# Four-layer attention kernel: one key block of each unit of the last layer has its exponentials computed on VectorE

## Chip, core and metric

The kernel runs on one core of a Trainium2 chip. The metric is the time of one execution on the device, in microseconds; the median of several executions is given. A profile is the record of one execution.

## The reference

Four layers follow each other on x, 2,048 rows of 640 numbers in bf16. Each adds to x an attention over its layer norm; layers 0 and 2 use a sliding window of 256 keys ("A"), layers 1 and 3 attend to all 2,048 keys ("B"). There are 32 heads of 20.

```python
def _B_ref(x, wqkv, wo):
    B, S, D = x.shape
    H = 32
    Dh = D // H
    qkv = (lambda x, *d: x.transpose(*d))((x @ wqkv).reshape(B, S, 3, H, Dh), 2, 0, 3, 1, 4)
    q, k, v = qkv[0], qkv[1], qkv[2]
    scores = jnp.einsum("bhqd,bhkd->bhqk", q, k) * (Dh ** -0.5)
    p = _softmax(scores, axis=-1)
    o = jnp.einsum("bhqk,bhkd->bhqd", p, v)
    return (lambda x, *d: x.transpose(*d))(o, 0, 2, 1, 3).reshape(B, S, D) @ wo
...
x = A_x
x = x + _A_ref(_layernorm(x, axis=-1), A_wqkv, A_wo)
x = x + _B_ref(_layernorm(x, axis=-1), B_wqkv, B_wo)
x = x + _A_ref(_layernorm(x, axis=-1), A_wqkv, A_wo)
x = x + _B_ref(_layernorm(x, axis=-1), B_wqkv, B_wo)
```

For the change one thing matters: every score of layer 3, 32 x 2,048 x 2,048 of them, needs an exponential.

## The kernel before, in words

**Units and banks.** The queries are split into NC = 4 chunks of C = 512, the heads into G = 8 groups of four. A unit (class Unit, L602) is a layer, a chunk c and a group g. In a full layer it has 16 key blocks of 128 keys, and for each block four banks, one per head j of the group: 64 banks of 128 keys x 512 queries, each as large as one PSUM bank. Layer 3's chunk 0 is split into two parts, which belong to the woven stage before; its chunks 1 to 3 are 24 whole units and are the end of the program.

**Scores, exponentials, values.** The main loop (L926) makes one tile of banks per tick. Score matmuls (L953) write it to PSUM: even ticks to banks 0 to 2, odd ticks to banks 3 to 5, or 3 to 6 if the tile has four banks. The four heads lie in different strips of 32 rows. One ScalarE instruction (L971) takes the exponential of the whole tile from PSUM to bf16 in SBUF, into a buffer pt of three banks, or, for four banks, into a slot of ka_all, whose 18 rows layer 3 no longer needs for keys (KA // 4 = 4 slots in turn). Two or three ticks later value matmuls (L1021) accumulate the four heads of one key block into PSUM bank 7, called op. The values have a column of ones, so row 20 of each strip becomes the sum of the exponentials.

**After a unit.** finish_unit (L760) copies op to oT on VectorE (L783), which frees bank 7 for the next unit. The tail t_tail (L803) makes the reciprocals of the sums and multiplies: four matmuls L808, reciprocal L813, split L817 and L818, transpose L823 and its copy L825, four matmuls L832, product L836. After the eighth unit of a chunk t_out (L500) projects: eight times eight matmuls (L511) and an add to x (L520). For the last chunk t_before_last (L534) does seven of each eight groups ahead (L542, L550). Each step of these tasks asks take_m (L235) for a free PSUM bank; in the last layer the only one is bank 6. The four-bank tiles use it too, when no task wants it (next_tile, L893).

**Order.** The order on every engine is that of emission, fixed when the program is built. A tick emits the scores of its tile, then the exponential, then as many steps of the tasks as a credit allows (pump, L223: 0.9 per tick in the last layer), then value matmuls of an earlier tile. Engines then wait for each other by semaphores. TensorE and VectorE each run their instructions in this order.

```python
                if n_b == 4:
                    pt = ka_all[:, 4 * wide_pt : 4 * wide_pt + 4, :]
                    wide_pt = (wide_pt + 1) % (KA // 4)
                else:
                    pt = ptp.tile([P, 3, C], BF16, name="pt", tag="pt")
...
                    nc.scalar.activation(
                        out=pt[:, i:k, b0 * P :], in_=sp[:, i:k, b0 * P :],
                        func=ACT.Exp, scale=SCALE,
                    )
```

Of the kernel before, what the change touches and what calls it, by code (L numbers as in the profile page):

```python
# [8 lines left out]

BF16 = mybir.dt.bfloat16  # L10
F32 = mybir.dt.float32
ALU = mybir.AluOpType
ACT = mybir.ActivationFunctionType

P = 128
# [4 lines left out]
NT = S // P  # L20
KD = D // P
G = 8
C = 512
NC = S // C
EPS = 1e-5
SCALE = DH ** -0.5
HD = D // 2
VW = DH + 1
KA = 18
QA = 4  # L30

PARTS = {
# [6 lines left out]
def kernel(  # L39
# [10 lines left out]
    nc = tc.nc  # L50
# [11 lines left out]
    xtp = pool("xtp", 5)  # L62
# [30 lines left out]
    ka_all = big.tile([P, KA, C], BF16, name="ka", tag="ka")  # L93
    kas = [ka_all[:, n, :] for n in range(KA)]
    qas = [big.tile([P, C], BF16, name=f"qa{n}", tag=f"qa{n}") for n in range(QA)]

    ps = psp.tile([P, 8, C], F32, name="ps", tag="ps")
    op = ps[:, 7, :]
# [15 lines left out]
    def load_wop(w):  # L114
# [6 lines left out]
        out=ident[:], in_=ident[:], compare_op=ALU.not_equal, fill=1.0,  # L121
# [101 lines left out]
    def pump(credit, most):  # L223
        state["credit"] = min(state["credit"] + credit, most)
        while True:
            t = choose(state["credit"] <= 0.0)
            if t is None:
                break
            state["credit"] -= advance(t)
# [369 lines left out]
    def key_blocks(l, part):  # L599
        return part or (0, NT)  # L600

    class Unit:  # L602
        def __init__(self, l, c, g, part=None):
            self.l, self.c, self.g, self.part = l, c, g, part
            self.windowed = l % 2 == 0
            if self.windowed:
                sets = [(m, b0, subs, j) for m, b0, subs in window_banks(c) for j in range(4)]
            else:
                kcs = range(*key_blocks(l, part))
                sets = [(None, 0, [(kc, 0, 4, 0)], j) for kc in kcs for j in range(4)]  # L610
            n = len(sets)
            self.banks = [
                (self, j, m, b0, subs, i < 4, i >= n - 4, i == n - 1)
                for i, (m, b0, subs, j) in enumerate(sets)
            ]

# [143 lines left out]
    def finish_unit(u):  # L760
# [22 lines left out]
            nc.vector.tensor_copy(out=oT[:], in_=op)  # L783
        push_tail(("tail", l, c, g), t_tail(l, c, g, on, oT))

    def s_emitted(u):
        if u.windowed:
            live["qa"] -= 1
            qa_free.append(qa.pop((u.c, u.g)))
            for c in ([u.c - 1] if u.c > 0 else []) + ([u.c] if u.c == NC - 1 else []):  # L790
                live["ka"] -= 1
                ka_free.append(ka.pop((c, u.g)))
        else:
            live["kt"] -= 1
            live["qt"] -= 1
# [69 lines left out]
    with tc.manual_schedule():  # L865
# [24 lines left out]
            starts.setdefault(id(b[0]), len(tiles) + m // 3)  # L890
        banks = deque(banks[n:])

        def next_tile(t):  # L893

            if t < len(tiles):
                return tiles[t]
            size = 3
            if t % 2 and not tails and state["held"] is None and mfree[6][0] <= state["tick"]:
                if all(task.wake > state["tick"] for task in todo):
                    size = 4  # L900
            return [banks.popleft() for _ in range(min(size, len(banks)))]
# [24 lines left out]
        while ended is None or t < ended + 8:  # L926
            t += 1
            state["tick"] += 1
            n_b = 0
            if t < len(tiles) or banks:  # L930
                cur = next_tile(t)
                n_b = len(cur)
                for b in cur:
                    u = b[0]
                    if id(u) not in started:
                        started.add(id(u))
                        if u.l == 0 and u.g == 0 and u.c + 1 < NC and u.c not in pushed:
                            pushed.add(u.c)
                            push(("stats", u.c + 1), t_stats0(u.c + 1), index[0, u.c + 1, 0, None], 0.4)
                            push_layer(0, u.c + 1)  # L940
                        state["unit"] = index[u.l, u.c, u.g, u.part]
                        state["act"] = state["unit"] < woven
                        if state["early"] and not narrow(u):
                            end_early()
                        start_unit(u)
                sp = ps[:, 0:3, :] if t % 2 == 0 else ps[:, 3:7, :]
                if n_b == 4:
                    mseq[0] += 1
                    mfree[6] = (state["tick"] + 2, mseq[0])
                for n in range(2):  # L950
                    for i, (u, j, m, b0, subs, first, last, end) in enumerate(cur):
                        for kc, q0, qn, col in subs[n : n + 1]:
                            nc.tensor.matmul(  # L953
                                sp[:, i, col * P : (col + qn) * P],
                                lhsT=u.k(kc, j), rhs=u.q(j, q0, qn), start=True, stop=True,
                            )
                for b in cur:
                    if b[-1]:
                        s_emitted(b[0])
                if n_b == 4:  # L960
                    pt = ka_all[:, 4 * wide_pt : 4 * wide_pt + 4, :]
                    wide_pt = (wide_pt + 1) % (KA // 4)
                else:
                    pt = ptp.tile([P, 3, C], BF16, name="pt", tag="pt")
                i = 0
                while i < n_b:
                    b0 = cur[i][3]
                    k = i
                    while k < n_b and cur[k][3] == b0:
                        k += 1  # L970
# [4 lines that stand above are left out]
                    i = k  # L975
                for i, b in enumerate(cur):
                    pts.append((t, pt, i, b))
                load_ahead()
                r = rate(t)
                pump(r, r + 0.1)  # L980
                state["heat"] += 0.414 * n_b
                work.append((state["heat"], 1.0 * n_b))
                if woven <= state["unit"] < index[3, 1, 0, None]:
                    least = sum(w[1] for w in work) - sum(w[0] for w in work) + state["heat"]
                    keep_clock(least)
                    work[-1] = (state["heat"], 1.0 * n_b)
                state["heat"] = 0.0
            else:
                ended = t if ended is None else ended
                pump(2.0, 2.0)  # L990

            if t > 0 and masked is not None:
                cur_, pt_ = masked
                i = 0
                while i < len(cur_):
                    m, b0 = cur_[i][2:4]
                    k = i
                    while k < len(cur_) and cur_[k][2] == m:
                        k += 1
                    if m is not None:  # L1000
                        mv_ = masks[:, m, b0 * P :].unsqueeze(1).to_broadcast(
                            (P, k - i, C - b0 * P)
                        )
                        nc.vector.tensor_tensor(  # L1004
                            out=pt_[:, i:k, b0 * P :], in0=pt_[:, i:k, b0 * P :], in1=mv_,
                            op=ALU.mult,
                        )
                    i = k
            masked = (cur, pt) if n_b else None

            if len(pts) >= 4 and pts[3][0] <= t - (3 if pts[0][3][0].windowed else 2):
                group = [pts.popleft() for _ in range(4)]
                u, subs, end = group[0][3][0], group[0][3][4], group[3][3][7]
                first, last = group[0][3][5:7]
                if first and u.windowed:
                    require(("v", u.l, u.c, 0))
                    require(("v", u.l, u.c, 1))
                for n, (kc, q0, qn, col) in enumerate(subs):
                    for _, pt, i, b in group:
                        j = b[1]  # L1020
                        nc.tensor.matmul(  # L1021
                            op[32 * j : 32 * j + VW, q0 * P : (q0 + qn) * P],
                            lhsT=u.v(kc, j), rhs=pt[:, i, col * P : (col + qn) * P],
                            start=(first and n == 0), stop=(last and n == len(subs) - 1),
                            skip_group_check=u.windowed,
                        )
                if end:
                    pv_emitted(u)
                    finish_unit(u)
# [35 lines left out]
```

## Time and profile before

| | |
|---|---|
| median of 4 runs | 2439.27 us (2432.26 to 2446.82) |
| profiled execution | 2443.57 us, its span 2441.6 us |
| TensorE matmul busy | 1996.4 us (82%) |
| TensorE weight load busy | 735.4 us (30%) |
| VectorE busy | 842.4 us (35%) |
| ScalarE busy | 2234.3 us (92%) |
| GpSimd busy | 134.1 us (5%) |
| mean granted TensorE clock | 0.824 |
| exponentials of three banks (and other small forms) | 1517, mean 1475 ns |
| exponentials of four banks | 140, mean 2125 ns |

How to read the profile: the span is cut into 40 slices, and each digit is the busy share of a slice in tenths; PEclk is the TensorE clock that was granted. A group of instructions has its line, engine, operation, output and input with their shapes, and a count; behind the first bar the busy time in us and the mean of one in ns, behind the second the time that the engine stood idle just before, and what ended it. In a timeline the columns are start and duration in us, engine, line, operation, tensors and count, and in brackets the idle time before with its releaser. A duration can include time in which the engine was still at the instruction before, so that durations of neighbours overlap.

### The profile page before, as it was taken

To read this page: it belongs to the slowest core of one execution; us is meant where nothing else is said; L and a number is where in the kernel's file an instruction comes from. 1 tells how busy PE (TensorE), PEld (TensorE's weight loads), DVE (VectorE), ACT (ScalarE), POOL (GpSimd) and SP (SyncE) were. 2 spreads that over 40 slices of the span, in tenths; PEclk is the share of its full clock that TensorE was granted. 3 is DMA by queue.
4 is the path that set the end of the run, shared out by engine and by line. 5 is a ranking of instruction groups with operands and counts; after the bars stand their busy time and mean duration, and the time that the engine had idled before them with its cause. 6 is when DMAs were issued, how large, how long until landed. Compare 5 with 4: busy or idle time off the path is not lost.

```text
span 2441.6 us, 39309 instructions
## 1 busy us (share of the span) xinstructions
PE 1996.4 (82%) x15738; PEld 735.4 (30%) x15738; DVE 842.4 (35%) x1920; ACT 2234.3 (92%) x1741; POOL 134.1 (5%) x278
## 2 busy tenths in 40 slices
PE   6888989888888888888888888888877787778777
PEld 2333333333322333333322333333322221122222
DVE  5676666523332344332443334452200010001001
ACT  5777788999989999999998989999999999999997
POOL 1111111010100001000010001001000000000000
PEclk9898999999889999999998989999855565556556
DMA  3223233231310124102230034122200010001100
GB/s 122 65 79 83 68 82 77 50 83 57 89 30 16 38 60 116 43 14 55 65 104 22 3 83 111 32 40 73 65 26 25 25 36 26 25 26 36 37 13 11
DMA packets 170823, 129.07 MB, mean 53 GB/s; under 512 B 115536, under 2 KB 153296, under 8 KB 170640
## 3 DMA queue, kind: packets, MB, share of 16 engines
q1 hardware_dynamic: 161904, 101.39, 16.3%
q0 software_dynamic: 8736, 25.18, 3.0%
q8 instruction: 123, 2.02, 0.3%
q14 instruction: 60, 0.49, 0.1%
HBM read 98.70 MB, written 27.79 MB: 52 GB/s over the span
## 4 chain that ended last, share of the span: by engine, by line
ACT 45%; PE 27%; issue 16%; DVE 8%; DMA 2%; SPq 1%; POOL 0%; ACTq 0%; DVEq 0%; POOLq 0%
ACT pt L971 37%; ACT ka L971 7%; PE ps L953 6%; PE ps L335 6%; PE ps L511 4%; PE ps L1021 4%; PE ps L593 3%; PE ps L426 3%; DVE pt L1004 2%; DVE st L286 1%; DMA wqk<-in_B_wqkv_dram 1%; DVE oT L783 1%; PE ps L390 1%; DVE on L836 1%; DVE x_sb L520 1%
## 5 line engine op out<-in xcount | busy, mean ns | idle before, releaser
L971 ACT ACTIVATE pt<-ps 128x1536 bf16<-128x1536 f32 (+5 forms) x1517 | 1998.1, 1475 | 157.4 <-PE ps L953 143.4
L953 PE MATMUL ps<-qt,kt 32*128 32x512 bf16 x4096 | 645.3, 467 | 287.7 <-ACT pt L971 174.6
L1021 PE MATMUL ps<-pt,vt 128*21 128x512 bf16 x3536 | 470.9, 448 | 8.7 <-DVE oT L783 6.0
L953 PEld LDWEIGHTS <-kt 32*128 32x128 bf16 x4096 | 199.3, 94 | 683.3 <-issue 667.5
L1004 DVE TENSOR_TENSOR pt<-pt,masks 128x1024 bf16<-128x1024 bf16 (+5 forms) x403 | 240.6, 625 | 166.7 <-ACT pt L971 165.7
L971 ACT ACTIVATE ka<-ps 128x2048 bf16<-128x2048 f32 x140 | 297.4, 2125 | 0.0
L335 PE MATMUL ps<-xnT,wqk 128*128 128x512 bf16 x830 | 228.9, 403 | 28.9 <-DMA wqk<-in_B_wqkv_dram 15.2
L593 PE MATMUL ps<-masks,ident 128*128 128x512 bf16 x764 | 231.3, 415 | 7.0 <-DVE st L286 2.8
L783 DVE CAST oT<-ps 128x512 bf16<-128x512 f32 x112 | 76.9, 687 | 458.8 <-PE ps L1021 458.8
L1021 PEld LDWEIGHTS <-vt 128*21 128x21 bf16 x4096 | 105.8, 91 | 324.8 <-issue 314.2
L511 PE MATMUL ps<-wop,on 128*128 128x320 bf16 x968 | 168.0, 314 | 6.2 <-DVE x_sb L520 3.9
L286 DVE CAST st<-ps 128x512 bf16<-128x512 f32 x127 | 87.7, 691 | 208.9 <-PE ps L335 208.5
L1021 PE MATMUL ps<-ka,vt 128*21 128x512 bf16 x560 | 147.8, 598 | 0.0
L953 PE MATMUL ps<-qa,ka 32*128 32x384 bf16 (+2 forms) x1408 | 117.9, 280 | 30.6 <-ACT pt L971 27.5
L836 DVE TENSOR_TENSOR on<-oT,ps 128x512 bf16<-128x512 bf16 x128 | 87.9, 686 | 141.8 <-PE ps L832 136.2
L426 PE MATMUL ps<-wv,xnT 128*128 128x320 bf16 x640 | 115.5, 315 | 7.5 <-DVE on L836 1.5
L520 DVE TENSOR_TENSOR x_sb<-x_sb,ps 128x320 bf16<-128x320 bf16 x120 | 58.2, 485 | 169.6 <-PE ps L511 169.4
L335 PEld LDWEIGHTS <-wqk 128*128 128x128 bf16 x830 | 72.2, 101 | 130.7 <-issue 55.4
L511 PEld LDWEIGHTS <-on 128*128 128x128 bf16 x968 | 88.2, 101 | 71.4 <-issue 38.5
L593 PEld LDWEIGHTS <-ident 128*128 128x128 bf16 x764 | 67.8, 102 | 113.7 <-issue 76.0
L1021 PE MATMUL ps<-pt,va 128*21 128x384 bf16 (+2 forms) x1408 | 80.3, 293 | 23.6 <-DVE oT L783 14.0
L813 DVE RECIPROCAL rz<-ps 128x16 f32<-128x16 f32 x128 | 32.7, 256 | 141.9 <-PE ps L808 141.2
(63 smaller groups left out, 881.8 us busy)
## 6 DMA issues: line engine op xcount, KB each, us to landing
vt<-v_d SPq DMA_DIRECT2D x48, 336.0 KB
kt<-k_d SPq DMA_DIRECT2D x192, 80.0 KB
wqk<-in_B_wqkv_dram SPq DMA_DIRECT2D x80, 160.0 KB
wqk<-in_A_wqkv_dram SPq DMA_DIRECT2D x70, 160.0 KB
k_d<-st POOLq DMA_DIRECT2D x75, 128.0 KB, 2.2
q_d<-st POOLq DMA_DIRECT2D x75, 128.0 KB, 2.1
qt<-q_d SPq DMA_DIRECT2D x384, 20.0 KB
v_d<-vs POOLq DMA_DIRECT2D x16, 336.0 KB, 3.5
```

The source lines that it names most:

```text
L286: nc.vector.tensor_copy(out=out_, in_=in_)
L335: nc.tensor.matmul(pq, lhsT=wt[:, dc, :], rhs=xt[:, dc, :], start=(dc == 0), stop=(dc == KD - 1),)
L426: nc.tensor.matmul(pv, lhsT=xt[:, dc, i * P : (i + 1) * P], rhs=wv_sb[l % 2][:, dc, h * HD : (h + 1) * HD], start=(dc == 0), stop=(dc == K ...
L511: nc.tensor.matmul(yp, lhsT=on[:, g, qb * P : (qb + 1) * P], rhs=wop[:, g, i * HD : (i + 1) * HD], start=(last or g == 0), stop=(g == G - 1),)
L520: nc.vector.tensor_tensor(out=xv, in0=had, in1=yp, op=ALU.add)
L593: nc.tensor.matmul(ps[:, b, :], lhsT=ident[:], rhs=masks[:, 0, :], start=True, stop=True)
L783: nc.vector.tensor_copy(out=oT[:], in_=op)
L836: nc.vector.tensor_tensor(out=on[:, g, :], in0=oT[:], in1=zb, op=ALU.mult)
L953: nc.tensor.matmul(sp[:, i, col * P : (col + qn) * P], lhsT=u.k(kc, j), rhs=u.q(j, q0, qn), start=True, stop=True,)
L971: nc.scalar.activation(out=pt[:, i:k, b0 * P :], in_=sp[:, i:k, b0 * P :], func=ACT.Exp, scale=SCALE,)
L1004: nc.vector.tensor_tensor(out=pt_[:, i:k, b0 * P :], in0=pt_[:, i:k, b0 * P :], in1=mv_, op=ALU.mult,)
L1021: nc.tensor.matmul(op[32 * j : 32 * j + VW, q0 * P : (q0 + qn) * P], lhsT=u.v(kc, j), rhs=pt[:, i, col * P : (col + qn) * P], start=(first ...
```

## The change

In layer 3's chunks 1 to 3, all units but the first, (1,0), are set "aside": 23 units. Such a unit leaves its last key block (four banks) out of the tiles. These banks go another way, two pairs per unit. For each bank one score matmul writes PSUM bank 6; VectorE reads it, scales it, adds the exponent bias and converts it to int32, in which the upper bits are the exponent of the power of two and the lower 23 its fraction. From the pair, 1,024 elements per partition, bit operations separate the two; a quartic in fp32 (a square of a square plus a linear term) gives two to the fraction, and a last multiply puts the power back. The result is stored as bf16 and enters the unit's accumulation as its last four value matmuls.

The buffers are four of the five xnT tiles, free by then, and six rows of ka_all; the four-bank tiles keep three slots in place of four. The emission is paced by a credit of its own (1.05 per tick, at most 1.2); a bank is started only in an odd tick, whose tile then has three banks. side_need makes the scores be emitted before the unit's keys are released, side_done the rest before the unit's last value matmuls.

```diff
+SIDE_RATE = 1.05
...
+            self.aside = False
...
+                self.aside = l == 3 and c > 0 and (c, g) != (1, 0)
+                k0, k1 = key_blocks(l, part)
+                kcs = range(k0, k1 - self.aside)
...
-                (self, j, m, b0, subs, i < 4, i >= n - 4, i == n - 1)
+                (self, j, m, b0, subs, i < 4, i >= n - 4 and not self.aside, i == n - 1)
...
+    def t_side():
+
+        xi, xm, xw, xe = side["tiles"]
+        V = nc.vector
+        while aside:
+            u = aside[0]
+            for pair in range(2):
+                while id(u) not in loaded:
+                    yield None
+                for i in range(2):
+                    yield "bank"
+                    mseq[0] += 1
+                    mfree[6] = (state["tick"] + 2, mseq[0])
+                    nc.tensor.matmul(
+                        ps[:, 6, :], lhsT=u.k(NT - 1, 2 * pair + i), rhs=u.q(2 * pair + i, 0, 4),
+                        start=True, stop=True,
+                    )
...
+                    V.tensor_scalar(
+                        out=xi.bitcast(I32)[:, i * C : (i + 1) * C], in0=ps[:, 6, :],
+                        scalar1=SCALE * LOG2E * E23, scalar2=127.0 * E23, op0=ALU.mult, op1=ALU.add,
+                    )
+                    yield 0.7
+                V.tensor_scalar(
+                    out=xm.bitcast(I32), in0=xi.bitcast(I32), scalar1=0x7FFFFF, scalar2=0x3F800000,
+                    op0=ALU.bitwise_and, op1=ALU.bitwise_or,
+                )
+                yield 0.7
+                V.tensor_scalar(
+                    out=xi.bitcast(I32), in0=xi.bitcast(I32), scalar1=-0x800000, scalar2=None,
+                    op0=ALU.bitwise_and,
+                )
+                yield 0.7
+                V.tensor_scalar(out=xe, in0=xi, scalar1=0.0, scalar2=None, op0=ALU.max)
+                yield 0.7
+                V.tensor_scalar(
+                    out=xm, in0=xm, scalar1=EK, scalar2=ES, op0=ALU.mult, op1=ALU.add
+                )
+                yield 0.7
+                V.tensor_tensor(out=xw, in0=xm, in1=xm, op=ALU.mult)
+                yield 1.2
+                V.tensor_scalar(out=xw, in0=xw, scalar1=EB, scalar2=None, op0=ALU.add)
+                yield 0.7
+                V.tensor_tensor(out=xw, in0=xw, in1=xw, op=ALU.mult)
+                yield 1.2
+                V.tensor_scalar(
+                    out=xm, in0=xm, scalar1=EC, scalar2=ED, op0=ALU.mult, op1=ALU.add
+                )
+                yield 0.7
+                while not side["out"]:
+                    yield None
+                pt = side["out"].popleft()
+                po = pt.rearrange("p a b -> p (a b)")
+                V.tensor_tensor(out=po, in0=xw, in1=xm, op=ALU.add)
+                yield 1.2
+
+                V.tensor_tensor(out=po, in0=po, in1=xe, op=ALU.mult)
+                side_out.setdefault(id(u), []).append(pt)
+                yield 0.7
+            aside.popleft()
...
+    def side_done(u):
+        n = 0
+        while len(side_out.get(id(u), ())) < 2:
+            n += 1
+            assert n < 10000
+            side["credit"] = max(side["credit"], 0.1)
+            if side_step(mfree[6][0] <= state["tick"]):
+                continue
...
+                side_now = (
+                    t % 2 and side["gen"] is not None and side.get("at") == "bank"
+                    and side["credit"] > 0.0 and mfree[6][0] <= state["tick"]
+                    and state["held"] is None
+                )
                 cur = next_tile(t)
...
+                if side_now:
+                    side_step(True)
...
-                    wide_pt = (wide_pt + 1) % (KA // 4)
+                    wide_pt = (wide_pt + 1) % 3
...
                 pump(r, r + 0.1)
+                side["credit"] = min(side["credit"] + SIDE_RATE, 1.2)
+                side_step(False)
...
+                if end and u.aside:
+                    pair = side_done(u)
+                    for j in range(4):
+                        nc.tensor.matmul(
+                            op[32 * j : 32 * j + VW, :], lhsT=u.v(NT - 1, j),
+                            rhs=pair[j // 2][:, j % 2, :], start=False, stop=True,
+                        )
+                    side["out"].extend(pair)
```

## Prediction

> **What bounds the kernel now.** The page first. Its rows of slices show two regimes: up to about 1,740 us VectorE is busy and the TensorE clock high, and after that only ScalarE is full.
>
> ```profile
> span 2441.6 us, 39309 instructions
> ...
> DVE  5676666523332344332443334452200010001001
> ACT  5777788999989999999998989999999999999997
> ...
> PEclk9898999999889999999998989999855565556556
> ...
> L971 ACT ACTIVATE ka<-ps 128x2048 bf16<-128x2048 f32 x140 | 297.4, 2125 | 0.0
> ```
>
> The last 11 slices (61 us each) are layer 3 from its second query chunk on. ScalarE is at 9 or more in nearly all, VectorE at 0 or 1, TensorE runs at about half clock. The group is the four-bank exponential, which exists only there. The table by stretches makes it exact (columns: stretch, its length, then busy us of PE, PEld, DVE, ACT, POOL, granted clock):
>
> ```profile
> 2050.00:2100.00 50.00, 36.82 (x247) 10.40 (x243) 4.40 (x12) 50.00 (x36) 0.00 (x0) 0.50 0.10 31
> 2100.00:2150.00 50.00, 37.66 (x247) 10.20 (x244) 4.40 (x12) 50.00 (x35) 0.00 (x0) 0.50 0.10 31
> ```
>
> ScalarE 50.0 of 50, VectorE 4.4. So whatever leaves ScalarE here shortens the stage, until another engine is late. The price of a bank is in ScalarE's timeline:
>
> ```profile
> 2101.71 1.97 ACT L971 ACTIVATE pt<-ps 128x1536 bf16<-128x1536 f32 x1
> 2103.05 2.40 ACT L971 ACTIVATE ka<-ps 128x2048 bf16<-128x2048 f32 x1
> 2104.82 1.97 ACT L971 ACTIVATE pt<-ps 128x1536 bf16<-128x1536 f32 x1
> 2106.22 2.34 ACT L971 ACTIVATE ka<-ps 128x2048 bf16<-128x2048 f32 x1
> ```
>
> Read starts, not durations (they overlap): a three-bank tile takes 1.34 us, a four-bank tile 1.77. The bank costs 0.43 and an instruction 0.05 more. VectorE's timeline of the same unit shows all that it does there:
>
> ```profile
> 2111.16 0.69 DVE L783 CAST oT<-ps 128x512 bf16<-128x512 f32 x1 [19.40 <-PE ps L1021]
> 2115.32 0.26 DVE L813 RECIPROCAL rz<-ps 128x16 f32<-128x16 f32 x1 [3.47 <-PE ps L808]
> 2115.62 0.17 DVE L817 CAST hl<-rz 128x16 bf16<-128x16 f32 x1
> 2115.83 0.17 DVE L818 TENSOR_TENSOR hl<-rz,hl 128x16 bf16<-128x16 f32 x1
> 2117.97 0.21 DVE L825 COPY rT<-ps 32x128 bf16<-32x128 bf16 x1 [1.97 <-PE ps L823]
> 2119.49 0.69 DVE L836 TENSOR_TENSOR on<-oT,ps 128x512 bf16<-128x512 bf16 x1 [1.31 <-PE ps L832]
> ```
>
> That is 2.2 us per unit, and an instruction that needs the one before starts 0.04 after its end (2115.58 to 2115.62). The oT copies run from 1765.38 (end of the chunk's first unit) to 2431.2 (the last): 23 units, 665.8 us, 28.95 us each.
>
> **What ScalarE loses.** Those 23 units each give up four banks: 92 x 0.427 = 39.3 us. TensorE's spare bank 6 is now taken by them, so of 140 four-bank tiles 65 are left. In the two programs, from the layer's second chunk on, this makes 465 exponentials into 459: six fewer, 0.3 us. Gain on the bounding engine **39.6 us**. TensorE does the same 92 score and 92 value matmuls, moved.
>
> **What VectorE gets.** Per pair of banks twelve instructions (two PSUM reads of 512, six one-source ones of 1,024 in SBUF, four two-source ones of 1,024), so 46 x 12 = 552. No fp32 SBUF row is in this trace; the nearest are these (behind the first bar busy us and the mean ns of one):
>
> ```profile
> L1004 DVE TENSOR_TENSOR pt<-pt,masks 128x1024 bf16<-128x1024 bf16 x132 | 89.2, 683 | 43.2 <-ACT pt L971 42.9
> ...
> L1004 DVE TENSOR_TENSOR pt<-pt,masks 128x512 bf16<-128x512 bf16 x134 | 54.5, 416 | 54.6 <-ACT pt L971 54.5
> ...
> L381 DVE TENSOR_SCALAR xn<-x_sb,rstd,nmr 128x640 bf16<-128x640 bf16 x64 | 28.6, 450 | 0.6
> ...
> L769 DVE TENSOR_TENSOR raw_o<-raw_o,ps 128x512 f32<-128x512 f32 x16 | 10.9, 680 | 1.0 <-PE ps L1021 1.0
> ```
>
> From 512 to 1,024 bf16 elements is 267 ns: two elements a cycle of 1.04 ns, and 149 ns fixed. The fp32 row with one PSUM input is 149 + 512 x 1.04: one a cycle. PSUM reads are therefore 0.69 us, as the oT copy is. A two-source fp32 instruction of 1,024: 149 + 1,067 = 1.22 us; the last multiply has an fp32 input and gets the same. (If it ran at two a cycle it would be 0.68, half a microsecond less a pair.)
>
> The one-source ones decide. L381 is the nearest row: (450 - 149)/640 = 0.47 ns, two bf16 elements a cycle. Carried over by bytes, fp32 would do one a cycle, 1.22 us. Against that stands the Trainium skill, page "VectorE: DVE Perf Modes", section "The perf-mode tier table (the rule you actually need)": an fp32 one-source operation with both ends in SBUF does two a cycle, 1,227 ns for 2,048 elements, while a two-source one does one. With its 2x and this trace's fixed part, 149 + 533 = 0.68 us. The page also gives bf16 one-source operations four a cycle, which L381 does not show (640 at four would be about 316 ns by this fixed part); its two per-partition scalars may be the reason, and the new instructions have constants. I take 0.68, and keep 1.22 as the far end.
>
> A pair: 2 x 0.69 + 6 x 0.68 + 4 x 1.22 + 12 x 0.04 = **10.8 us** by the page, **14.0** by the row. A unit: two pairs, 2.2 of tail, eight residual adds of 0.49 per eight units (0.5), their gaps 0.2: **24.5 us** or **30.9**. The shortened unit lasts 28.95 - 39.6/23 = 27.2. So VectorE is 90% full by the one and too slow by the other.
>
> **New waits, and their cover.** VectorE's reads of bank 6 wait for TensorE's side matmul; behind them in its queue stand the rest of the chain, the oT copy (TensorE's next unit needs bank 7), and the tail's PSUM reads. In the trace the oT copy ended at 2111.85 and the next unit's value matmuls began at 2112.27: 0.42 spare. TensorE then had 0.26 before its next scores, and a score matmul set ends 0.6 or so before ScalarE needs it. About 1.3 us of delay is hidden, as much as one side instruction in progress. The emission is paced at ten tiles a pair, in bits of 0.7 to 2.2 us per 1.34 us tile, so the queue is seldom more than 1 us behind. I charge 2 us in all; if that cover were gone it would be one 1.2 us instruction a unit, 28 us.
>
> The value matmuls of the side bank wait for the last multiply. By the emission order they have it one or two tiles ahead up to unit (3,4); at (3,5) and (3,6) one and two instructions are pushed out at that very point, 1.3 and 2.5 us less the cover: **3 us** with what was already queued.
>
> The output projections need bank 6 too. Before, a projection of eight groups came in bursts of 5 and 3. By the emission order it is now broken into three, four to six tiles apart. The start of a burst at half clock costs ScalarE most:
>
> ```profile
> 1977.30 1.45 ACT L971 ACTIVATE pt<-ps 128x1536 bf16<-128x1536 f32 x1 [1.03 <-PE ps L953]
> 1979.14 2.97 ACT L971 ACTIVATE pt<-ps 128x1536 bf16<-128x1536 f32 x2 [0.39 <-PE ps L953]
> ```
>
> Two more starts of 1.03 in each of three projections: **6 us**. The added residual adds do not queue: between two of them (1.84 us) one side instruction fits.
>
> At the end, five of the last pair's instructions are emitted only when the value matmuls ask for them: two one-source (0.72 with the gap) and three two-source (1.26), 5.2 us. From that pair's second PSUM read VectorE has 10.1 us and some adds of 0.49, about 12; ScalarE's remaining tiles take 5.5 to 7 from there. So it is 5 us late, and three groups of the "before last" projection (1.1 us each) now fall behind it, 2 us on the path, less 1 us that they no longer take from ScalarE: **6 us**.
>
> At nothing: the four xnT tiles are borrowed after all projections are done; the three-slot ring of wide tiles is reused after six tiles, when the value matmuls are two or three behind; no DMA is added on any queue, and no side bank delays the release of keys (no score is pushed out late).
>
> Sum: 39.6 - 2 - 3 - 6 - 6 = **22.6 us**. The profiled run took 2443.57 (span 2441.6 and 2.0 around it), 4.3 above the median; the saving is a count of banks, the same on either. From the profiled time it gives 2421, from the median of 2439.27 **2417 us**.
>
> **The rivals.** A measurement of this kernel tells 0.5%, 12.2 us, from no change: faster is below 2427, slower above 2451.
>
> *VectorE becomes the bound (slower).* Place: the six one-source instructions of t_side. At one element a cycle a unit needs 30.9 us against 28.95 now: 23 x 1.95 = +45, **2484 us**. It turns to a loss where a pair costs over (28.95 - 2.9)/2 = 13.0 us. For it: L381's 0.47 ns. Against: the page's row, and the constants. 17%.
>
> *Handoffs through bank 6 and bank 7 cost a unit one instruction.* At 90% full, VectorE's queue is long when oT or a reciprocal arrives; 0.7 us beyond the cover, 23 times, is 16 us more: **2433**, no change that can be told. For it: TensorE is in order, so a wait on VectorE holds the next scores too. Against: 1.3 us of cover. 17%.
>
> *Nearly all arrives.* Projection bursts raise the clock sooner and cover is enough, so only the end's 6 us are lost: 33.6 saved, **2406**. For it: ScalarE was never late for anything but projections (11.6 us in 22 waits). 16%.
>
> *The forecast*, 2417 within about 8: 50%. The change cannot fail to do what it says: the programs differ by just those 92 banks.
>
> The range takes in full gain and the handoff case up to the edge of the loss: 2402 to 2446, which leaves out the loss and little else. Faster 0.67 (forecast, full gain), same 0.16, slower 0.17.
>
> **What would show it.** In the profile after: one-source side instructions at 680 ns and two-source at 1,220; VectorE near nine tenths in the last ten slices; three-bank exponentials still 1.33 apart; 65 four-bank ones; ScalarE idle for TensorE rising from 11.6 us to about 22; a unit of 27.7 us; a tail 6 us longer between the last exponential and the end. One-source at 1.2 us makes the prediction wrong at its root. ScalarE waiting in every unit right after the oT copy, or TensorE scores that wait for VectorE's read of bank 6, would be the handoff case.

## The result, and the profile after

The changed kernel takes 2428.8 us (median of 43 runs, 2419.7 to 2441.1) against 2439.3 for the kernel before (64 runs). The ratio is 0.996, 95% interval 0.9951 to 0.997: a gain of 9.8 us (7.3 to 12.0), under half of the 22.6 that were forecast. It lies within 0.5%, though its sign is certain.

The page of the kernel after:

```profile
span 2433.3 us, 39979 instructions
...
DVE  5676756433332344332343334452577777777776
...
PEclk9898999999889999999998989999855565556556
...
L1135 ACT ACTIVATE ka<-ps 128x2048 bf16<-128x2048 f32 x65 | 127.3, 1958 | 2.6 <-PE ps L1115 2.2
```

VectorE went from 0 or 1 to 7 tenths in the last slices, not to the foretold nine. The four-bank exponentials fell from 140 to the foretold 65. The two stretches of the prediction again (length, then busy us of PE, PEld, DVE, ACT, POOL, granted clock):

```profile
2050.00:2100.00 50.00, 41.94 (x261) 9.88 (x253) 36.18 (x54) 49.72 (x36) 0.00 (x0) 0.50 0.10 31
2100.00:2150.00 50.00, 40.76 (x255) 10.02 (x251) 38.46 (x55) 49.17 (x36) 0.00 (x0) 0.50 0.11 31
```

ScalarE is still at 49.2 to 49.7 of 50, so it still bounds the stage, and VectorE has 12 to 14 us of every 50 free. The kernel nevertheless gave back 31 of the 40 us that ScalarE was relieved of. Three of VectorE's new rows first, in the last layer alone (busy us and mean ns behind the first bar):

```profile
L870 DVE TENSOR_TENSOR ka<-xnT 128x1024 bf16<-128x1024 f32 x46 | 56.2, 1222 | 1.1
...
L858 DVE TENSOR_SCALAR xnT<-xnT 128x1024 f32<-128x1024 f32 x46 | 31.8, 691 | 1.1
L873 DVE TENSOR_TENSOR ka<-ka,xnT 128x1024 bf16<-128x1024 bf16 x46 | 31.7, 689 | 1.2
```

The prices are those of the forecast or lower. A pair has 9.87 us of busy time by all its rows, 10.3 with the gaps, against 10.8. So the cost is not in what VectorE does but in when. The waits of the last layer (us in total, times, longest):

```profile
ACT pt L1135 <- PE ps L1115: 24.3, 26, 2.0
...
PE ps L1187 <- DVE oT L797: 10.2, 15, 1.7
...
PE ps L1196 <- DVE ka L873: 6.2, 2, 4.5
```

The kernel before has this for the first line, and nothing like the second and the third:

```profile
ACT pt L971 <- PE ps L953: 11.6, 22, 1.1
```

Now TensorE waits 15 times for the copy of the finished unit's accumulator. One of those, in the timeline of TensorE, VectorE and ScalarE:

```profile
1903.80 0.69 DVE L850 TENSOR_SCALAR xnT<-xnT 128x1024 bf16<-128x1024 f32 x1
...
1904.40 0.69 DVE L852 TENSOR_SCALAR xnT<-xnT 128x1024 f32<-128x1024 f32 x1
...
1905.01 0.68 DVE L797 CAST oT<-ps 128x512 bf16<-128x512 f32 x1
...
1905.74 0.61 PE L1187 MATMUL ps<-pt,vt 128*21 128x512 bf16 x4 [1.58 <-DVE oT L797]
...
1907.00 5.48 ACT L1135 ACTIVATE pt<-ps 128x1536 bf16<-128x1536 f32 x4 [1.15 <-PE ps L1115]
```

The unit's last value matmuls were over at about 1903.6. The copy was emitted behind one PSUM read and four one-source side instructions of 0.69 us, which had piled up within two tiles, and began 1.4 us later. TensorE's next value matmuls need the copy; in TensorE's queue the next scores stand behind them; and ScalarE stood 1.15 us. From then on its exponentials are again 1.34 us apart: the four shown take 5.48 us, the last of them 1.45, and (5.48 - 1.45)/3 is 1.34.

The end has two parts. In the kernel before the last exponential ended at 2430.56; the copy and the product on of the last unit were these:

```profile
2431.25 0.69 DVE L783 CAST oT<-ps 128x512 bf16<-128x512 f32 x1 [6.40 <-PE ps L1021]
...
2434.30 0.69 DVE L836 TENSOR_TENSOR on<-oT,ps 128x512 bf16<-128x512 bf16 x1 [0.67 <-PE ps L832]
```

In the kernel after, behind ScalarE's last exponential, which ended at 2408.57:

```profile
2415.05 0.69 DVE L873 TENSOR_TENSOR ka<-ka,xnT 128x1024 bf16<-128x1024 bf16 x1
2415.80 0.60 PE L1196 MATMUL ps<-ka,vt 128*21 128x512 bf16 x2 [4.50 <-DVE ka L873]
...
2416.43 0.69 DVE L797 CAST oT<-ps 128x512 bf16<-128x512 f32 x1 [0.69 <-PE ps L1196]
...
2418.96 2.03 PE L553 MATMUL ps<-wop,on 128*128 128x320 bf16 x7 [0.58 <-DVE raw_o L561]
...
2425.95 0.69 DVE L987 TENSOR_TENSOR on<-oT,ps 128x512 bf16<-128x512 bf16 x1 [0.67 <-PE ps L983]
```

TensorE waits 4.5 us for the last pair; the last oT copy begins at 2416.43, 7.9 us after the last exponential where it was 0.7. After that the tail takes 9.5 us from copy to product where it took 3.05, because projection groups of 2.03 us (seven matmuls L553 each) stand in it. The granted clock around that wait (the number behind the five busy times):

```profile
2411.00:2415.80 4.80, 0.30 (x7) 0.00 (x1) 4.64 (x6) 0.00 (x0) 0.00 (x0) 0.86 0.00 0
2416.30:2425.90 9.60, 7.21 (x32) 3.62 (x30) 2.97 (x8) 0.00 (x0) 0.00 (x0) 0.50 0.00 0
```

**The balance.** Let each exponential's end follow the last by 0.0525 us and 0.4267 per bank; what is over that is ScalarE's loss. Summed from the layer's second chunk on, by place:

| us | before | after | change | forecast |
|---|---|---|---|---|
| fewer banks and instructions on ScalarE | | | -39.6 | -39.6 |
| ScalarE's loss at the three projections | 11.0 | 21.2 | +10.2 | +6 |
| at the projection before the last | 4.2 | 2.1 | -2.1 | -1 |
| at unit ends and elsewhere | 4.7 | 13.7 | +9.0 | +5 |
| last exponential to end of span | 11.1 | 24.7 | +13.6 | +7 |
| sum | | | -8.9 | -22.6 |

The span fell by 8.3 us (2441.6 to 2433.3), and 0.5 of the difference lies ahead of this stage, so the balance is complete to 0.1 us.

The 13.7 us at unit ends and elsewhere, put to their places in the trace: 4.4 are differences under 0.05 us each, as before (4.7). 3.0 stand right behind four oT copies. 1.7 follow one late last multiply, at unit (3,6), for which TensorE waited 1.7 us. And 3.9 stand in the middle of eleven units, where a four-bank tile waits until the tail's product on has read bank 6. The rest is 0.7.

### The profile page after: what moved, and what is told of

It reads as the page before. It is cut to its first block, busy times and chain, and to the rows that moved or that the text cites. A ratio compares the mean times of both kernels' runs of the same rounds, so it can differ in the third digit from the quotient of the medians.

```text
span 2433.3 us, 39979 instructions
## 1 busy us (share of the span) xinstructions
PE 2025.6 (83%) x15738; PEld 728.8 (30%) x15738; DVE 1274.4 (52%) x2472; ACT 2196.5 (90%) x1735; POOL 134.1 (6%) x278
## 3 DMA queue, kind: packets, MB, share of 16 engines
q8 instruction: 123, 2.02, 0.3%
## 4 chain that ended last, share of the span: by engine, by line
ACT 37%; PE 29%; issue 17%; DVE 13%; DMA 2%; SPq 1%; POOL 0%; ACTq 0%; DVEq 0%; POOLq 0%
ACT pt L1135 34%; PE ps L1115 7%; PE ps L346 5%; PE ps L1187 4%; PE ps L522 4%; PE ps L604 3%; ACT ka L1135 2%; PE ps L437 2%; DVE pt L1170 2%; DMA wqk<-in_B_wqkv_dram 1%; DVE on L987 1%; DVE st L297 1%; DVE oT L797 1%; PE ps L401 1%; DVE x_sb L531 1%
## 5 line engine op out<-in xcount | busy, mean ns | idle before, releaser
L1135 ACT ACTIVATE pt<-ps 128x1536 bf16<-128x1536 f32 (+3 forms) x1586 | 2053.1, 1444 | 171.1 <-PE ps L1115 155.6
L1115 PEld LDWEIGHTS <-kt 32*128 32x128 bf16 x4004 | 189.5, 94 | 634.3 <-issue 616.4
L522 PE MATMUL ps<-wop,on 128*128 128x320 bf16 x968 | 173.9, 322 | 7.0 <-DVE x_sb L531 4.1
L1115 PE MATMUL ps<-qa,ka 32*128 32x384 bf16 (+2 forms) x1408 | 117.0, 278 | 30.2 <-ACT pt L1135 27.2
L835 DVE TENSOR_SCALAR xnT<-ps 128x512 int32<-128x512 f32 x92 | 63.5, 691 | 128.7 <-PE ps L829 125.5
L1135 ACT ACTIVATE ka<-ps 128x2048 bf16<-128x2048 f32 x65 | 127.3, 1958 | 2.6 <-PE ps L1115 2.2
L976 DVE COPY rT<-ps 32x128 bf16<-32x128 bf16 x128 | 26.7, 209 | 92.5 <-PE ps L974 91.8
```

The lines of the kernel that those rows point to most:

```text
L522: nc.tensor.matmul(yp, lhsT=on[:, g, qb * P : (qb + 1) * P], rhs=wop[:, g, i * HD : (i + 1) * HD], start=(last or g == 0), stop=(g == G - 1),)
L1115: nc.tensor.matmul(sp[:, i, col * P : (col + qn) * P], lhsT=u.k(kc, j), rhs=u.q(j, q0, qn), start=True, stop=True,)
L1135: nc.scalar.activation(out=pt[:, i:k, b0 * P :], in_=sp[:, i:k, b0 * P :], func=ACT.Exp, scale=SCALE,)
```

## The experiments

Two theories were open for the 14 us that the forecast lacked. One, H where a letter stands for it: handoffs, that is, short instructions that others wait for stand behind side work in VectorE's queue, and the last pair has no cover. The other, B: it is the breaking-up of the projections, whose bursts each start with TensorE at half clock. The kernel after is the base of every edit. A ratio is always to the kernel before on the same chip, which takes 2432.8 to 2439.9 us on these chips; differences between runs on different chips are taken from the ratios, times 2439.3. The ratios of e1, e2, e5 and e6 are known only to within 6 to 9 us either way, so they do not by themselves tell the two theories apart; the traces do. The stage from the last woven unit's copy to the end of the span, in one profile each:

| | before | after | e1 | e2 | e3 | e5 | e6 |
|---|---|---|---|---|---|---|---|
| us | 708.8 | 700.0 | 689.9 | 688.4 | 679.6 | 692.5 | 683.3 |

**e1: the last unit keeps all its banks on ScalarE.**

```diff
-                self.aside = l == 3 and c > 0 and (c, g) != (1, 0)
+                self.aside = l == 3 and c > 0 and (c, g) not in ((1, 0), (NC - 1, G - 1))
```

> The last unit (3,7) keeps all its banks on ScalarE; 22 units stay aside. Theory H (the missing gain is TensorE waiting for VectorE, most of it at the end of the program): the stretch from the last exponential to the end falls from 24.7 us to about 11 as in the kernel before, so 13.7 us back, less 1.7 for four banks and about 2 because the whole of the before-last projection is taken from ScalarE again: 2419 us. Theory B (the missing gain is bank 6: projections broken into more bursts at half clock): nothing of that changes here but the before-last projection; at most 3 us back: 2426 us.

2418.0 us, ratio 0.9929 (0.9902 to 0.9956), which is 2422 on the scale of the forecast, between the two. Last exponential to end of span is 11.1 us again. The end alone, 13.6 us, cost more than the whole change had gained; 1.7 of it go back to the four banks on ScalarE and 1.7 to the projection before the last (3.8 us of loss, 2.1 in the kernel after).

**e2: as e1, and also the first unit of each chunk stays whole, and no side bank is started while a projection is open**, so that projections run in bursts as before.

```diff
+                self.aside = l == 3 and c > 0 and g > 0 and (c, g) != (NC - 1, G - 1)
...
-                    and state["held"] is None
+                    and state["held"] is None and not todo
```

> The first unit of each chunk and the last unit keep all banks on ScalarE (20 units aside in place of 23), and a side bank is started only when no projection is pending, so the projections are bursts of 5 and 3 groups again. Theory B: the projections' excess over the nominal time of the exponentials falls from 21 us to the 11 of the kernel before, and the end to 11 us; 10 + 13.7 back, 5.1 lost for twelve banks and 2 for the before-last projection: 2412 us. Theory H alone (breaking the projections up costs nothing): only the end comes back: 2422 us.

2416.9 us, 0.9918 (0.9888 to 0.9948): between the two. It has eight banks fewer aside than e1 (3.4 us of ScalarE) and its stage is still 1.5 us shorter. ScalarE's loss at the three projections is 4.4, 5.6 and 5.2 us; in the kernel after it is 5.7, 9.5 and 6.0. Undoing the breaking-up is worth about 4.9 us.

**e3: the side chain cut to three of its twelve instructions.** It leaves out the splitting and the quartic, so that its side banks are not exponentials; emission, pacing and TensorE's work are those of the kernel after.

```diff
-                V.tensor_scalar(
-                    out=xm.bitcast(I32), in0=xi.bitcast(I32), scalar1=0x7FFFFF, scalar2=0x3F800000,
...
+                for cost in (0.7, 0.7, 0.7, 0.7, 1.2, 0.7, 1.2, 0.7):
+                    yield cost
...
-                V.tensor_tensor(out=po, in0=xw, in1=xm, op=ALU.add)
...
-                V.tensor_tensor(out=po, in0=po, in1=xe, op=ALU.mult)
+                V.tensor_scalar(out=po, in0=xi, scalar1=0.0, scalar2=None, op0=ALU.max)
```

> Of the twelve VectorE instructions of a pair nine are left out (the splitting of the bits and the quartic); the two reads of PSUM and one last instruction stay, so the output is not the reference's. The emission, its pacing, bank 6 and TensorE's work are as in the changed kernel. Theory H: no instruction is long in front of an oT copy or of the last value matmuls any more; about 9 us of waits at unit ends and 5 of the 13.7 us at the end go: 2414 us. Theory B: the projections stay broken up, and nothing else was lost: 2426 us.

2412.3 us, 0.99 (0.9871 to 0.9929), as H has it. TensorE's waits for oT fall from 10.2 to 2.3 us. It also separates terms: at the projections ScalarE's loss is 17.1 us (5.4, 5.7 and 5.9), 6.1 over the kernel before, and that is the breaking-up alone. The unit ends lose 5.3, as good as before. The end stays 6.4 us longer, mostly by the projection groups; 0.65 us are a wait of TensorE for the thin chain's own last instruction:

```profile
2394.98 0.39 PE L1171 MATMUL ps<-ka,vt 128*21 128x512 bf16 x2 [0.65 <-DVE ka L848]
...
2395.41 0.69 DVE L797 CAST oT<-ps 128x512 bf16<-128x512 f32 x1 [0.48 <-PE ps L1171]
...
2397.01 1.11 PE L553 MATMUL ps<-wop,on 128*128 128x320 bf16 x7 [0.58 <-DVE raw_o L561]
...
2401.91 0.69 DVE L962 TENSOR_TENSOR on<-oT,ps 128x512 bf16<-128x512 bf16 x1 [0.47 <-PE ps L958]
```

From copy to product 6.5 us, where 3.05 were before, with the groups at 1.11 us; in the kernel after the same groups take 2.03 and the same stretch 9.5. TensorE had stood still for 0.65 us here, not 4.5, and the clock granted from 2391.6 to 2402 was 1.00.

**e4: a pair of 14.0 us**, the max done six times, as if one-source instructions had cost what row L381 suggested.

```diff
-                V.tensor_scalar(out=xe, in0=xi, scalar1=0.0, scalar2=None, op0=ALU.max)
+                for _ in range(6):
+                    V.tensor_scalar(out=xe, in0=xi, scalar1=0.0, scalar2=None, op0=ALU.max)
```

> One of the one-source instructions of 1,024 fp32 elements (the maximum with zero) is done six times in place of once: a pair costs 10.3 + 5 x 0.73 = 14.0 us on VectorE, as the prediction's slower rival has it. That rival's rule: a unit needs 2 x 14.0 + 2.9 = 30.9 us against 28.95 in the kernel before, so slower than both kernels, 2484 us. If VectorE has more room than that sum says (its waits can be moved into it), about 2440 us.

2561.5 us, 1.0518 (1.0475 to 1.0561): far above both. VectorE is busy in only 647.6 us of the stage's 804. By the forecast's sum a full VectorE would have given 2484; the waits around it gave another 77.

**e7: the max done three times, a pair of 11.8 us** (`range(3)` in the same place).

> The changed kernel with the maximum with zero done three times in place of once: a pair costs 10.3 + 2 x 0.73 = 11.8 us on VectorE, a unit 2 x 11.8 + 2.9 = 26.5 us, still below the 27.7 us that a unit lasts. If VectorE costs nothing until it is full (the rule of the prediction, loss from 13.0 us a pair on): 2430 us. If its queue is what TensorE waits for long before that (theory H): a third to a half of the way to e4, 2470 us.

2470.0 us, 1.0133 (1.0092 to 1.0175). The stage by busy time:

```profile
1724.00:2436.00 712.00, 546.23 (x3478) 145.71 (x3478) 554.69 (x809) 649.51 (x458) 0.00 (x0) 0.55 0.09 27
```

VectorE 554.7 of 712, 78%, and the kernel loses about 32 us against before. Its load costs long before it is full.

**e6: e2, and the side work of a tile emitted behind its value matmuls and the copy**, no longer ahead of them.

```diff
                 pump(r, r + 0.1)
-                side["credit"] = min(side["credit"] + SIDE_RATE, 1.2)
-                side_step(False)
...
                     finish_unit(u)
+            if n_b:
+                side["credit"] = min(side["credit"] + SIDE_RATE, 1.2)
+                side_step(False)
```

> As e2_chunk_starts_whole, and the side instructions of a tile are emitted behind that tile's value matmuls and the oT copy in place of ahead of them, so that in VectorE's queue the copy has one tile's instructions fewer in front. Theory H: TensorE's wait for the copy (9.7 us in 13 waits in e2) falls to about half, and ScalarE's idle time at unit ends from some 9 us to 4: 2412 us where e2 has 2417. If these waits come from an instruction already running, not from the order: unchanged, 2417 us.

2409.3 us, 0.9893 (0.9857 to 0.9929): 26 us faster than before, the best of all here, and it leaves nothing of the computation out. The waits for oT, in e2 and in e6:

```profile
PE ps L1187 <- DVE oT L797: 9.7, 13, 1.7
...
PE ps L1185 <- DVE oT L797: 1.1, 3, 0.6
```

Nothing but the place of the emission was changed between the two. The intervals of their times overlap, so it is the waits that show the effect; ScalarE's loss at unit ends and elsewhere fell from 13.9 to 10.9 us, where the kernel before has 4.7. What is left stands for the most part before four-bank tiles that wait for the product on.

**e5: only this move, on the kernel after.**

> The changed kernel with all its 23 units aside and its broken-up projections, only with the side instructions of a tile emitted behind the value matmuls and the oT copy. Theory H: TensorE's 10.2 us of waits for the copy go, about 6 us of it seen by ScalarE; at the end three instructions are late in place of five and one projection group lies behind the last value matmuls in place of three, 6 us; one instruction more is late at units (3,4) to (3,6), 3 us lost: 2420 us. If the order in VectorE's queue is not the cause: 2429 us as the changed kernel.

2424.2 us, 0.9936 (0.9912 to 0.996), between the two expectations: waits for oT fall to 3.7 us. The interval overlaps that of the kernel after, so the time alone would not have shown it; the wait does. But ScalarE's whole loss ahead of the end hardly changes (36.3 us, 37.0 in the kernel after), since the projection before the last loses 5.8 us where it lost 2.1. What is gained lies at the end: TensorE waits 2.6 us for the last pair, not 4.5, and the last exponential to the end of the span is 17.9 us, not 24.7.

Next, whether VectorE's load would be free in e6's order.

**e10: e6 with the max done three times.**

> As e6_side_behind_copy, with the maximum with zero done three times in place of once (11.8 us a pair, as in e7). If e7's 39 us were the order in VectorE's queue, most of them stay away here: 2418 us, 9 more than e6. If they are VectorE's capacity, which is used up at 11.8 us a pair although its busy share is under 80%: 20 units in place of 23 pay, 34 us more than e6: 2443 us.

2445.2 us, 1.0032 (1.0014 to 1.005). Not free. TensorE waits 19.5 us for rT (0.8 in e6), and ScalarE 25.4 us at 17 four-bank tiles (3.4 at 11 in e6). Here the three max instructions are emitted in one lump, which is a possible cause, so:

**e12: the work of e10, with the two copies at two places, each with a pause of its own, and faster pacing** (1.35 per tile, at most 1.5).

```diff
-SIDE_RATE = 1.05
+SIDE_RATE = 1.35
...
+                V.tensor_scalar(out=xe, in0=xi, scalar1=0.0, scalar2=None, op0=ALU.max)
+                yield 0.7
...
+                yield 0.7
+                V.tensor_scalar(out=xe, in0=xi, scalar1=0.0, scalar2=None, op0=ALU.max)
```

> As e10, with the same work (11.8 us a pair), but the two added copies of the maximum with zero stand at two places of the chain and are paid for in the pacing like every other instruction (credit 1.35 per tile, at most 1.5), so that they are not emitted in one lump. If e10's 33 us over e6 come from the lump, in front of the tails' short steps: most of it goes, 2416 us. If they are VectorE's capacity: as e10, 2443 us.

2439.6 us, 1.0011 (0.9993 to 1.0029). That is no clear gain over e10; but the pacing was changed as well, which needs its own run:

**e13: e6 with the faster pacing alone**, no instruction added.

> As e6_side_behind_copy, with the pacing of e12 (credit 1.35 per tile, at most 1.5) and the chain of the changed kernel. More instructions are emitted per tile, so the queue in front of a copy or a tail's step can be longer. If the shape of the emission matters as much as the amount: 4 to 8 us over e6, 2416 us. If not: 2410 us.

2444.4 us, 1.0033 (1.0017 to 1.0049). This went against both expectations: the same instructions as e6, only sooner, cost 34 us. So e12 against e10 says nothing of spreading. But e12 against e13, on one chip, does: with 80 instructions of 0.69 us more (40 pairs, two each) and a pause for each of them, e12 took no longer than e13, 4.7 us less by the medians. Where most of the 34 us are, in e13's timeline:

```profile
1864.19 1.23 DVE L870 TENSOR_TENSOR ka<-xnT 128x1024 bf16<-128x1024 f32 x1
1865.33 0.68 DVE L987 TENSOR_TENSOR on<-oT,ps 128x512 bf16<-128x512 bf16 x1
...
1866.06 0.58 PE L1115 MATMUL ps<-qt,kt 32*128 32x512 bf16 x1 [1.83 <-DVE on L987]
...
1866.68 1.88 ACT L1135 ACTIVATE ka<-ps 128x2048 bf16<-128x2048 f32 x1 [2.12 <-PE ps L1115]
```

The tail's product on reads bank 6, and stands behind two side instructions emitted in the tile before (one of them shown). The next four-bank tile wants bank 6 for its fourth bank, so TensorE waits 1.83 us and ScalarE 2.12. The waits of ScalarE at four-bank tiles of the last layer, in e13 and in e6:

```profile
ACT ka L1135 <- PE ps L1115: 27.1, 17, 2.2
...
ACT ka L1135 <- PE ps L1115: 3.4, 11, 0.5
```

That is 24 of the 34 us; another 10 are at three-bank tiles (24.3 us in e13, 14.7 in e6).

**e14: e13, but no side step in a tile ahead of one in which the tail may emit.**

```diff
-                side_step(False)
+                if all(x.wake > state["tick"] + 1 for x in tails):
+                    side_step(False)
```

> The faster pacing (1.35 per tile, at most 1.5), with the same work as the version whose side work stands behind the copy, and one rule more: in a tile ahead of one in which the tail may emit a step, no side step is emitted. By the order of emission rT is then followed at once by the product on, where the faster pacing had two side instructions (0.68 and 1.22 us) between them. If the tail's reads of bank 6 standing behind side work are what the faster pacing lost (27.1 us of ScalarE waiting at four-bank tiles), those waits all but vanish and the time is about 2416. If the loss is of another kind, VectorE's total work or the sooner start of each pair, it stays at about 2440.

2467.6 us, 1.0125 (1.0075 to 1.0175): slower still, which neither case had. The waits of its last layer:

```profile
ACT pt L1135 <- PE ps L1115: 76.1, 38, 6.5
...
PE ps L1194 <- DVE ka L873: 60.3, 11, 6.9
...
DVE rz L964 <- PE ps L959: 33.9, 22, 2.6
```

The waits before four-bank tiles are gone, as the reading of e13 had it. But VectorE now stands idle for the tail's inputs: 33.9 us for the reciprocals, and 29.4 and 27.8 for rT and on in the same view. The pair is then late at the other end, and TensorE waits 60.3 us for last multiplies before value matmuls. The cure for one deadline missed the other.

**e16: e14 with the max done three times**, in exactly the same order of emission.

> The kernel with the faster pacing and the tail let first, and in each pair the max done three times (two more one-source instructions, 1.5 us a pair, 65 us of VectorE in the stage): the order of emission is exactly the same, so the difference between the two is the price of VectorE's load alone. If load is free as long as VectorE is not full (it would be busy about 530 of 680 us), at most 8 us more than its light partner. If load costs as it did in the other orders, 30 to 40 us more, about 2450.

2492.9 us, 1.023 (1.0187 to 1.0274), 25 us over e14 on the same chip, between the two cases. Three pairs of kernels differ by this load alone. It is two instructions of 0.69 us and 0.04 of gap for each pair of banks: about 67 us on VectorE for the 46 pairs of e7, and 58 for the 40 pairs of e10 and e16, not the 65 of the expectation. The price is from the ratios times 2439:

| order of emission | VectorE busy in the stage with the load | load | price of the load |
|---|---|---|---|
| the kernel after (e7) | 78% | 67 us | 42 us |
| e6 (e10) | 72% | 58 us | 34 us |
| e14 (e16) | 68% | 58 us | 25 us |

## Why the prediction was wrong, point by point

**The gain, 39.6 us, held; the costs did not.** By the balance the forecast had 13.7 us too many: 6.6 at the end, 4.2 at the projections, 4.0 at unit ends, less 1.1 at the projection before the last. Exponentials stand 1.34 us apart as before, 65 have four banks, and ScalarE is still the bound.

**VectorE's prices held, with one miss in its favour.** The one-source instructions take 683 to 694 ns, int32 bit operations too: the doubled rate that the Trainium skill's page "VectorE: DVE Perf Modes", section "The perf-mode tier table (the rule you actually need)", gives fp32 one-source operations in SBUF, with this trace's fixed part. Row L381 was the wrong guide. The last multiply was priced at 1.22 us because its factor xe was taken for fp32; it is bf16 and took 0.689. The foretold nine tenths of VectorE came out as 7, in part for that reason, and because gaps were counted as busy and a unit lasted 28.3 us, not 27.2.

**The first step that failed is the cover at a unit's end**: "About 1.3 us of delay is hidden, as much as one side instruction in progress", and "the queue is seldom more than 1 us behind". A PSUM read and four one-source instructions came within two tiles and stood ahead of the copy. Unit ends lost 9.0 us, not 5: the late last multiplies 1.7 of the 3 foretold for them, and the queue about 7.3 where the cover left it 2. Of these, 3.0 stand behind the copies; e6 shows that cause by changing the order alone (9.7 to 1.1 us of waits for oT). The 3.9 before four-bank tiles have another: the product on is late too, and the tile's fourth bank waits for bank 6, which it reads. The forecast's charge does not name that path; its handoff rival does ("TensorE scores that wait for VectorE's read of bank 6"). This share was read from the trace, and e13, where it grew, agrees.

**The second, and the largest miss, is the end**: +13.6 us for 7. The thin chain (e3) has 6.4 of it, of which 0.65 are still a wait for its pair; so the last pair's lateness is about 7.8 us. Of these, about 4.8 are plain delay (5 were foretold). About 3.0 are clock: that is how much longer copy to product takes after than in e3. TensorE had stood 4.5 us and its groups then took 2.03 us, not 1.1; nothing in the forecast had that. (The kernel before has a clock of 0.51 in its tail too, from 2430.5 to 2434, but no projection groups there.) The projection groups moved behind cost about 5.8, not 2: four and part of a fifth are left when ScalarE ends, not three, and one follows another by 1.7 us even at full clock (2395.30 to 2397.01 in e3), since the add must first free bank 6; they delay both the last value matmuls and the tail. e1 got all of the end back (11.1 us).

**The third is the size of the projections; their mechanism was right.** The breaking-up costs 6.1 us with a thin chain, 6 were foretold. The other 4.1 us of +10.2 come with the full chain, which is all that differs from e3, and 3.8 of them lie at one projection, the second (9.5 us after, 5.7 in e3). The trace has no queue of residual adds there: TensorE waits 0.54 us for the product on ahead of the first group, and 0.26 at most for an add. What differs is the clock. It rose some 6 us after that group's start, in e3 after 4, and between the bursts it fell back: 1.00 from 1975 to 1977, 0.50 from 1978 to 1984, where e3 kept 1.00 from 1964 to 1984. So groups of eight matmuls took 2.31 and 2.02 us, not 1.26. How the full chain brings the clock down is not shown.

**The rivals.** Handoffs (2433) was the nearest in time, and in sign: waits right after the copy. It had named its mechanism but not the end, which cost more: it put 16 us more than the forecast at the unit ends, where 4.0 more were lost, so the nearness of its number is luck. "VectorE becomes the bound" did not come true, but its threshold was wrong as well: a loss was to begin at pairs of over 13.0 us, yet at 11.8 the kernel lost 32 us. It compared sums of busy time, as if VectorE could do its work in any order. Its chain has two ends that TensorE waits for, and short instructions in between that TensorE also waits for.

**What stays open.** In the three orders where nothing else was changed, the load costs 25 to 42 us of its 58 or 67. e12 took it up at e13's pace without losing time, so the price is not one of VectorE's capacity alone; whether e6's order, the fastest, can take it free is not shown. Why e14's side work does not catch up after the tail was read from its waits, not tested by a run.

## What to carry to other kernels

An idle engine that takes over work is not judged by its busy share: list the short instructions that others wait for on it (here the copy oT, rT, the product on, the last multiply) and count what is emitted ahead of each. Then put the long work behind them, as e6 does, emit it no faster than it is needed, as e13 did not, and check that its own last instruction is still in time, as e14's was not. The last unit of a program has nothing behind it that hides lateness, so it takes no such work.

## What the runs showed of the hardware that was not expected

- Within 5 us a stalled TensorE lost its clock: 0.86 on average from 2411.0 to 2415.8, 0.50 after, and the same groups of seven matmuls took 2.03 us for 1.11. In e3, where the groups kept TensorE busy for 7.0 of 10.4 us in the same stretch, the clock stayed at 1.00. A standstill is not needed for such a loss: in the kernel before TensorE was busy for about 1.6 us from 2426 to 2430, with no pause over 1.4 us, and the clock went from 1.00 to 0.50 by 2431.
- The same instructions, at the same place in the emission of a tile, took 0.9893 of the time of the kernel before in e6 and 1.0033 in e13, by the pace of emission alone.
